# Gate fold in column groups, last rows of the busiest expert in token order, second layer as nested arms, new sort keys

## Chip, cores and metric

One NeuronCore of a Trainium2 chip. The metric is the device time of one launch in microseconds (us); the kernel before has a median of 461.15 us over 3 runs (461.02 to 465.25).

## The reference

A block-sparse attention (2 batches, 8 heads, 768 positions, head size 64) gives 1536 token rows of 512 values. Two layers follow:

```python
def _moe_ref(x, w1, w2, w3, w_out):
    h = np.maximum(np.maximum(x @ w1, x @ w2), x @ w3)      # 512 -> 768
    return h @ w_out                                        # 768 -> 512

def _moe2_ref(x, w_skip, w_gate, w1, w2):
    do_compute = x @ w_skip > 0
    out = x.copy()
    e_idx = np.argmax(x @ w_gate, axis=1)                   # one of 8 experts
    gate_w = softmax(x @ w_gate)[chosen]
    for e in range(8):                                      # rows of expert e that compute
        h = np.maximum(x[mask] @ w1[e], 0.0)                # 512 -> 1024
        out[mask] = x[mask] + gate_w * (h @ w2[e])          # 1024 -> 512
```

On the inputs as drawn, the reference sends 1379 tokens to the busiest expert, 130 to a second one and 14 to a third; 13 skip the second layer. Of the 1379, 1252 lie ahead of the last 128 tokens.

## The kernel before, in words

**First stage (0 to 296 us of the span).** The 1536 tokens are worked in four groups `u` of 384. For each group there is attention over four head pairs (scores on PE, L301; softmax on DVE, ACT and POOL; transposes, L340; product with v, L353), then 18 `chain`s (L412: 12 matmuls of 384 columns each, three for each of six column blocks `f` of the hidden layer, from high and low parts of weights and input), their maximum on DVE (`chained`, L421), a split into high and low parts (`h_high` on ACT, `h_low` on POOL), and `x2_mm` (L439), which gives the 512 outputs and, in ten more columns, the logits of the second layer's gate. For these ten columns w_out is multiplied by the gate's weights beforehand, for each of six blocks `f` of w_out: `fold_t` transposes the block (L477), `fold_c` copies it to SBUF, `fold_mm` multiplies it with `w9` (L488: four matmuls of 10 columns in true float32, which are 8 passes in the trace), `fold_h` and `fold_l` split the result into the two weights.

The order of all of this is made by `arrange`, a list scheduler that runs when the kernel is built: each operation has an engine, a duration, dependencies, buffers, and a key from the table `KEYS`; of what is ready on an engine, that with the smallest key goes next. `HOME` says which copies run on another engine than ACT. Three PSUM buffers (`pm`) are shared by the chains, `x2_mm`, the folds and the routing. The 16 chunks of the first expert's weights are split into high and low parts on ACT (L774) and DVE (L776) at the end of this stage.

**Routing.** `route`, `route2`, `route3` find for each token its expert, its gate weight and its slot in a table in DRAM (`table`, CAP rows for each expert); `guess` picks the busiest expert from the counts of the first three groups.

**Second layer (296 us to the end).** The busiest expert's tokens are worked in `pair`s of two tiles of 128 rows, gathered by indirect DMA from `x2d`, and scattered to `out` by indirect DMA (`end`, L1108, POOL). `pair(0, 0)` and `pair(0, 1)` run under `tc.If(EA > EARLY)` (L1233). Beside the first of them DVE works `steps()` of `plan()`: some fifty small instructions on one partition that give the numbers of tiles, the experts' order and the rows to gather, for the registers of the engines. After the two arms of that If have joined, a second If (L1315) picks `most()` (one large expert, a few small ones) or `any_ranks()` (anything else). `most()` runs `pair(0, b0 + 1, 1)` and `pair(0, b0 + 2, FAST2)`, which carry the up to 32 left-over rows of two small experts as `tail`s (matmuls with a 32-column weight in four column groups, L1063 and L1074), then by `If`s on the count VK[0] further pairs (L1298, L1300), a `single` tile of 128 rows for an odd count (L1302) and a `single` of the second expert (L1304).

On these inputs the trace shows five pairs and two singles, twelve scatters in all: 11 tiles of the busiest expert and one of the second, in that order the last two being `single(0, l0)` and `single(1, b1 + 1)`. `single` has a first layer of 24 matmuls of 512 columns (L1185), transposes of the hidden rows (L1191), and a second layer of 24 matmuls of 512 columns (L1215); after it `end(1)` multiplies by the gate weight and adds the token row (L1105) and scatters.

Of the kernel before, what the change touches and what calls it, by code (L numbers as in the profile page):

```python
# [42 lines left out]
MAXT = NT  # L43
NRAW = 4
NCON = 293
# [7 lines left out]
KIND = dict(ch=0, cp=0, x2m=0, sc=1, pv=2, tu=3, st=3, ft=3, fm=1, wu=5)  # L53
PORTED, SWITCH = 0.5, 0.06

KEYS = dict(
    s=[[92.73, -181.27, -146.9, -16.72], [12.35, 16.72, 8.44, 74.05], [153.96, 186.16, 209.64, 168.62],
       [133.34, 186.33, 278.0, 31.35]],
    t=[[-48.88, -30.72, -72.46, -64.96], [-115.16, -107.84, -74.91, -96.18], [166.13, 294.76, 153.99, 200.69],
       [231.34, 228.77, 194.22, 148.78]],  # L60
    o=[[-192.26, -99.49, -155.84, -140.77], [18.47, 16.47, 41.51, 37.81], [199.26, 186.19, 169.77, 161.26],
       [233.93, 202.13, 203.99, 188.4]],
    v=[[-76.04, -20.69, -43.67, -52.86], [-21.73, 66.33, 25.77, 62.78], [184.33, 170.84, 129.72, 69.28],
       [217.41, 88.27, 101.06, 155.42]],
    d=[[-190.77, -106.26, -79.61, -70.3], [14.18, 17.1, 46.42, 50.54], [166.48, 205.9, 182.89, 208.26],
       [219.14, 230.09, 253.13, 240.15]],
    e=[[-118.48, -161.65, -267.53, -240.31], [-154.8, -98.57, -105.32, -102.62], [120.29, 131.21, 115.09,
       112.64], [172.38, 173.49, 165.52, 214.6]],
    c=[[23.72, 3.57, 54.8, 22.22, 44.87, 43.88, 88.26, 54.59, 86.07, 36.89, 6.99, -26.57, -32.31, 15.28,
# [5 lines left out]
    x=[-95.61, 258.36, 184.11, 502.78],  # L75
    w=[18.99, -6.3, 51.7, 43.13, 14.1, 99.04, 74.8, 61.7, 81.52, 99.86, 64.82, 35.29, 63.01, 76.52, 58.72,
       87.44, 90.17, 111.95, 78.35, 139.2, 88.06, 51.57, 155.3, 161.2],
    l=[-91.01, -34.87, 30.81, -0.24, -49.37, 13.11, 15.41, -9.33, 19.62, 18.83, 49.47, 74.71, 132.91, 84.56,
       70.49, 102.42, 139.84, 87.62, 100.63, 192.14, 145.35, 197.7, 185.22, 170.88],
    f=[61.9, 116.3, 154.03, 120.79, 115.82, 130.96],  # L80
# [11 lines left out]
def arrange(ops, room, keys):  # L92
# [46 lines left out]
    while len(order) < len(ops):  # L139
# [13 lines left out]
        for e in free:  # L153
            while free[e] <= now + 1e-9 and ready[e]:
# [7 lines left out]
                if e == "PE":  # L162
                    begin += SWITCH if kind not in (None, KIND.get(k, 4)) else 0.0
                    kind = KIND.get(k, 4)
# [29 lines left out]
def build(tc, a, out):  # L194
# [975 lines left out]
    def single(p, t, spl=0, last=False, hr=HR):  # L1170
# [31 lines left out]
        for f in range(8):  # L1202
            wh, wl = M2["w", p, 8 + f]
            i, o = f // 4, f % 4 * P
            if f == 2:
                turn_h(1)
                if not last:
                    turn_x()
# [171 lines left out]
```

## Time and profile before

| | |
|---|---|
| median of 3 runs | 461.15 us |
| profiled execution | 461.57 us, span 459.8 us |
| PE busy | 436.2 us, 95% of the span |
| DVE, ACT, POOL busy | 239.1, 187.7, 146.8 us |
| mean granted clock of TensorE | 0.988 of full speed |
| first stage / second layer | 0 to 296 / 296 to 459.8 us |

The span is the time between the first and the last recorded instruction; 1.8 us of the profiled execution lie outside of it. A matmul's end is modelled, so the pace of PE is read from the starts of consecutive matmuls. "Idle before" is time in which an engine had nothing to run, with the event that ended it.

### The profile page before, as it was taken

The numbers are of one execution on the slowest core, as the hardware profiler recorded it, in microseconds if no ns is written. First come the engines' busy times: TensorE is split into PE (matmuls) and PEld (weight loads), VectorE is DVE, ScalarE is ACT, GpSimd is POOL, SyncE is SP. The second block draws the span as 40 slices with busy tenths as digits, with TensorE's granted clock in tenths as the row PEclk, the third lists the DMA queues.
The fourth block names the chain that finished last, engine by engine and source line by source line (L and its number), as shares of the span: only waits on it lengthen the run. The fifth ranks groups of instructions, "written<-read, shape, count | busy, mean of one in ns | idle before, by whom it ended". The sixth has DMA issues, their size and how long they took to land. (4 is left out here: it accounts for less than half of the span.)

```text
span 459.8 us, 9575 instructions
## 1 busy us (share of the span) xinstructions
PE 436.2 (95%) x3523; PEld 392.3 (85%) x3523; DVE 239.1 (52%) x708; ACT 187.7 (41%) x505; POOL 146.8 (32%) x199
## 2 busy tenths in 40 slices
PE   6999899999999899999999998999989999999992
PEld 2767789999999898999999997999969889798881
DVE  3689899999832833325204168575136551323220
ACT  2688886555462767623211065211115511111220
POOL 2464456325121532104400251142224043231230
PEclk9799999999999999999999999999999999999998
DMA  8964635678203444501012074324911381010100
GB/s 253 296 223 138 228 117 184 210 239 265 70 17 138 144 86 143 177 16 47 2 61 78 2 265 150 137 45 120 341 49 50 94 301 68 19 50 20 55 18 29
DMA packets 27670, 56.85 MB, mean 124 GB/s; under 512 B 6463, under 2 KB 8767, under 8 KB 27608
## 3 DMA queue, kind: packets, MB, share of 16 engines
q1 hardware_dynamic: 24808, 49.71, 33.3%
q0 software_dynamic: 2800, 6.37, 4.4%
q8 instruction: 32, 0.52, 0.6%
q14 instruction: 30, 0.25, 0.2%
HBM read 46.95 MB, written 10.47 MB: 125 GB/s over the span
## 5 line engine op out<-in xcount | busy, mean ns | idle before, releaser
L412 PE MATMUL pm<-xh,wh 128*128 128x384 f32 x288 | 65.4, 347 | 1.3 <-DVE t L421 1.1
L412 PE MATMUL pm<-xl,wh 128*128 128x384 f32 x288 | 62.4, 336 | 0.3 <-DVE xl L364 0.3
L412 PE MATMUL pm<-xh,wl 128*128 128x384 f32 x288 | 62.4, 336 | 0.0
L412 PEld LDWEIGHTS pm<-xh,wh 128*128 128x128 f32 x288 | 49.6, 188 | 3.6 <-DVE t L421 2.1
L1133 ACT ACTIVATE hth<-ph 128x256 fp32r<-128x256 f32 x40 | 15.4, 385 | 89.6 <-PE ph L1130 82.2
L412 PEld LDWEIGHTS pm<-xl,wh 128*128 128x128 f32 x288 | 51.2, 188 | 0.7 <-DVE xl L364 0.7
L412 PEld LDWEIGHTS pm<-xh,wl 128*128 128x128 f32 x288 | 51.2, 188 | 0.0
L1134 DVE SCALAR_TENSOR_TENSOR htl<-ph,hth 128x256 fp32r<-128x256 f32 x40 | 16.8, 423 | 61.9 <-ACT hth L1133 60.8
L439 PE MATMUL pm<-wh,h 128*128 128x262 f32 (+1 forms) x288 | 42.3, 287 | 1.9 <-ACT h L426 0.7
L335 POOL TENSOR_TENSOR pr<-pr,se 128x360 f32<-128x360 f32 x32 | 26.5, 845 | 55.2 <-DVE se L331 44.8
L421 DVE TENSOR_TENSOR t<-pm,t 128x384 f32<-128x384 f32 x48 | 26.4, 551 | 31.8 <-PE pm L412 22.7
L325 ACT ACTIVATE pr<-pr,mx 128x120 f32<-128x120 f32 x96 | 36.6, 384 | 14.6 <-DVE mx L318 14.5
L439 PEld LDWEIGHTS pm<-wh,h 128*128 128x128 f32 x288 | 38.0, 189 | 2.9 <-ACT h L426 0.9
L429 POOL TENSOR_TENSOR h<-t,h 128x384 fp32r<-128x384 f32 x24 | 26.2, 1099 | 35.3 <-ACT h L426 26.7
L756 POOL DMA_INDIRECT xn<-x2d,inx x16 | 17.7, 1103 | 52.5 <-DVE xm L1096 24.2
L1142 PE MATMUL pm<-wh,hth 128*128 128x512 f32 x80 | 31.8, 397 | 0.0
L1142 PE MATMUL pm<-wh,htl 128*128 128x512 f32 x80 | 31.5, 393 | 0.0
L1142 PE MATMUL pm<-wl,hth 128*128 128x512 f32 x80 | 31.3, 391 | 0.0
L600 POOL DMA_INDIRECT table<-rtab,rsi x12 | 12.0, 1001 | 54.6 <-DVE g_m L617 20.9
L1130 PE MATMUL ph<-xth,wh 128*128 128x256 f32 x160 | 26.3, 286 | 2.1 <-issue 2.1
L1130 PEld LDWEIGHTS ph<-xth,wh 128*128 128x128 f32 x160 | 23.1, 188 | 4.6 <-issue 2.9
L388 POOL TENSOR_SCALAR cx<-cx 128x512 f32<-128x512 f32 x24 | 19.2, 803 | 21.4 <-ACT cx L384 21.1
(295 smaller groups left out, 847.8 us busy)
## 6 DMA issues: line engine op xcount, KB each, us to landing
raw<-in_m SPq DMA_DIRECT2D x48, 256.0 KB
raw<-in_wx SPq DMA_DIRECT2D x22, 512.0 KB
vx<-in_vx SPq DMA_DIRECT2D x14, 288.0 KB
qt<-in_qt SPq DMA_DIRECT2D x16, 192.0 KB
raw<-in_vt SPq DMA_DIRECT2D x8, 384.0 KB
x2d<-raw SPq DMA_DIRECT2D x12, 256.0 KB
kx<-in_kx SPq DMA_DIRECT2D x8, 360.0 KB
out<-raw SPq DMA_DIRECT2D x9, 256.0 KB
```

Source lines behind the costliest of these rows:

```text
L325: nc.scalar.activation(pr[:, t, :], pr[:, t, :], AF.Exp, bias=mx[:, t:t + 1], scale=-1.0, accum_out=se[:, h, t:t + 1])
L335: nc.gpsimd.tensor_tensor(pr, pr, ST["se", u, p][:, h].unsqueeze(2).broadcast_to([P, TPG, KT]), ALU.mult)
L388: nc.gpsimd.tensor_scalar(x, x, HIGH, LOW, ALU.min, ALU.max)
L412: nc.tensor.matmul(ST["ch", u, f, j], l[j, f][:, c * P:(c + 1) * P], r[u][:, c, :], start=(cs[0] == 0 and n == 0), stop=(cs[-1] == KC1 - 1 ...
L421: nc.vector.tensor_tensor(ST["t1", u, f], ps, ST["t1", u, f], ALU.max)
L429: nc.gpsimd.tensor_tensor(HL[u, f], ST["t1", u, f], HH[u, f].bitcast(F32), ALU.subtract)
L439: nc.tensor.matmul(ps, l[u, f][:, t * P:(t + 1) * P], r[3, f][:, lo:hi], start=(part != 1 and n == 0), stop=(part != 0 and n == len(ops) - 1))
L756: nc.gpsimd.indirect_dma_start(out=xn[t], out_offset=None, in_=x2d, in_offset=bass.IndirectOffsetOnAxis(ap=inx[:, t, 0:1], axis=0), bounds ...
L1130: nc.tensor.matmul(ps, w[:, o:o + P], r[:, d, :], start=(n == 0), stop=(n == 3 * KC1 - 1))
L1133: nc.scalar.activation(hh, ps, AF.Relu)
L1134: nc.vector.scalar_tensor_tensor(hl, ps, 0.0, hh.bitcast(F32), ALU.max, ALU.subtract)
L1142: nc.tensor.matmul(py[i], l[:, o:o + P], r, start=(f == 0 and n == 0), stop=(f == 7 and n == 2))
```

## The change

Four parts, and a table of numbers.

1. `fold_mm` multiplies in four column groups of 32: each of the four pieces of the contraction writes its own 32 rows of one PSUM tile (128 columns). `fold_s` copies that to SBUF on ACT, and `fold_q` adds the four pieces by one matmul with the constant `pick9`. `fold_h` and `fold_l` follow as before.
2. The last 128 tokens are a tile in SBUF already. Where leaving them out of the count of the busiest expert saves a tile, the last tile of that expert is replaced by these 128 tokens in token order (`dense`): they are transposed during the second expert's `single`, all 128 are computed, a mask (by slot) sets the gate weight to zero for those that the regular tiles hold, and two plain stores of 256 columns write the rows. The rows of `out` are read first. The table's steps on DVE grow for it.
3. `most()` stands inside the first If, behind `pair(0, 1)`; one word (`ints[:, 6 * NE:]`) holds all that its arms need, and the arms are nested, each with its own copy of what follows, so that one path through them lies in a row. `any_ranks()` stands in the program twice.
4. New `KEYS` and `HOME`; in the scheduler's model a change of PE from one kind of work to another costs more.

Core of the diff (the tables are shown by one line each):

```diff
-    o=[[-192.26, -99.49, -155.84, -140.77], [18.47, 16.47, 41.51, 37.81], [199.26, 186.19, 169.77, 161.26],
+    o=[[-117.16, -89.93, -97.28, -83.95], [25.53, 37.54, -54.69, 32.04], [110.79, 140.86, 128.76, 119.48],
...
-    ("c4", "Pool"): [0, 1, 3, 6, 8, 9, 14, 17, 21, 22, 23],
-    ("fv", "Pool"): [(0, 1), (0, 2), (0, 3)],
+    ("c4", "Pool"): [0, 2, 6, 8, 9, 18, 20, 21],
+    ("fv", "Pool"): [(0, 0), (0, 1), (0, 2), (0, 3)],
+    ("ph", "DVE"): [(0, 0), (1, 1)],
...
     def fold_mm(f):
         pg = psM.tile([P, 512], F32, name="pm")
         for c in range(KC1):
-            nc.tensor.matmul(pg[:, :NG9], ST["ft", f][:, c * P:(c + 1) * P], w9[:, c, :], start=(c == 0),
-                             stop=(c == KC1 - 1))
+            nc.tensor.matmul(pg[32 * c:32 * c + 32, :P], con[:, c * NG9:c * NG9 + 32], ST["ft", f][:, c * P:(c + 1) * P], start=True, stop=True)
+    def fold_s(f):
+        nc.scalar.copy(ST["ft", f][:, :P], ST["fg", f][:, :P])
+    def fold_q(f):
+        ST["fg", f] = ST["fg", f][:, 2 * P:]
+        nc.tensor.matmul(ST["fg", f][:, :NG9], ST["ft", f][:, :P], pick9, start=True, stop=True)
...
+    def turn_d():
+        nc.vector.memset(yq[:1], 1.0)
+        for c in range(KC1):
+            o = slice(c * P, (c + 1) * P)
+            nc.tensor.transpose(ptx[0][:, o], X2[NG - 1, TPG - 1][:, o], ident)
+    def put_d():
+        src = ptx[0].rearrange("p (c k) -> p c k", k=P)
+        nc.scalar.copy(xth[:, :, :P], src)
+        nc.vector.tensor_tensor(xtl[:, :, :P], src, xth[:, :, :P].bitcast(F32), ALU.subtract)
+    def gate_d():
+        nc.tensor.matmul(pq[:, :2], yq[:1], ONE["lim"], start=True, stop=True)
...
+    def second_d(z, f):
+        wh, wl = M2["w", 0, 8 + f]
+        h, o = f // 4, f % 4 * P
+        for n, (l, r) in enumerate(((hth[h], wh), (hth[h], wl), (htl[h], wh))):
+            nc.tensor.matmul(py[z][:, halves[z]], l[:, o:o + P], r[:, halves[z]],
+                             start=(f == 0 and n == 0), stop=(f == 7 and n == 2))
+    def end_d():
+        rows = out[B * S - P:, :]
+        nc.sync.dma_start(xr[1], rows)
+        for z, cs in enumerate(halves):
+            for f in range(4, 8):
+                second_d(z, f)
+            nc.vector.scalar_tensor_tensor(yo[0][:, cs], py[z][:, cs], gd[1], xr[1][:, cs], ALU.mult, ALU.add)
+            nc.sync.dma_start(rows[:, cs], yo[0][:, cs])
...
-        with tc.If(VK[0] > 6):
-            pair(0, b0 + 3)
-            with tc.If(VK[0] > 8):
-                pair(0, b0 + 4)
-        with tc.If((VK[0] & 1) == 0):
-            single(0, l0, hr=M2["raw"])
-        with tc.If(VK[1] > 1):
-            single(1, b1 + 1, last=True, hr=M2["raw"])
+        def last():
+            with tc.If((w & DENSE) > 0, preferred_fallthrough_block=True) as dense:
+                single(1, b1 + 1, last=True, hr=M2["raw"], then=True)
+                single(0, 0, last=True, hr=M2["raw"][2:], dense=True)
+            with dense.Else():
+                with tc.If((w & ONES) > 0):
+                    single(1, b1 + 1, last=True, hr=M2["raw"])
+        def odd():
+            with tc.If((w & 1) > 0, preferred_fallthrough_block=False) as one:
+                single(0, l0, hr=M2["raw"])
+                last()
+            with one.Else():
+                last()
+        with tc.If((w & (ONES - 1)) > 5, preferred_fallthrough_block=True) as four:
+            pair(0, b0 + 3)
+            with tc.If((w & (ONES - 1)) > 7, preferred_fallthrough_block=False) as five:
+                pair(0, b0 + 4)
+                odd()
+            with five.Else():
+                odd()
...
+    with tc.If(EA > EARLY, preferred_fallthrough_block=True) as early2:
+        with tc.manual_schedule():
+            pair(0, 0, gen=steps())
+            numbers()
+            pair(0, 1)
+            word = reg(ints[:, 6 * NE:], 2 * OTHER - 1)
+            with tc.If(word >= OTHER, preferred_fallthrough_block=False) as others:
+                any_ranks()
+            with others.Else():
+                most(word)
```

How the instructions move. On PE, what stands between the end of `pair(0, 1)` (or of the other arm) and the first matmul of the next pair, before: the last matmul of the pair, a jump over the whole other arm (whose last rows are the two transposes and two jumps), then the loads of registers and the second If.

```order
L1142 MATMUL pm<-wh_5_3761,htl_3982 128x512
L1233 UNCONDITIONAL_BRANCH
...
L743 MATMUL ptx_3488<-ident,xn_3490 128x128 x4
L1240 UNCONDITIONAL_BRANCH
L1233 UNCONDITIONAL_BRANCH
L732 TENSOR_LOAD p_ints
L1315 COMPARE_AND_BRANCH
L732 TENSOR_LOAD p_ints x2
L1130 MATMUL ph_3484<-xth,wh_0_3535 128x256
```

The same place now, word for word in a row of the program:

```order
L1185 MATMUL pm<-wh_5_3771,htl_4000 128x512
L772 TENSOR_LOAD p_ints
L1411 COMPARE_AND_BRANCH
L1173 MATMUL ph_3516<-xth,wh_0_3569 128x256
L1173 MATMUL ph_3516<-xth,wh_0_3650 128x256
```

One load and one compare are left, and no jump. The second place is PE behind `pair(0, b0 + 3)`, before (with the jumps that end the Ifs behind the pair that isn't run):

```order
L1142 MATMUL pm<-wh_5_3761,htl_3982 128x512
L1300 UNCONDITIONAL_BRANCH x2
L1298 UNCONDITIONAL_BRANCH
L1302 REGISTER_ALU
L1302 COMPARE_AND_BRANCH
L1185 MATMUL ph_3484<-wh_0_3535,xth 128x512
```

and now (L1266 is the first layer of the second expert's `single`):

```order
L1185 MATMUL pm<-wh_5_3771,htl_4000 128x512
L1389 REGISTER_ALU
L1389 COMPARE_AND_BRANCH
L1381 REGISTER_ALU
L1381 COMPARE_AND_BRANCH
L1373 REGISTER_ALU
L1373 COMPARE_AND_BRANCH
L1266 MATMUL ph_3516<-wh_5_3928,xth 128x512
```

Three compares stand here, and the arm that this word selects follows them directly. The third place is DVE at the end of the first stage (L421, now L424, is the maximum that frees a chain's PSUM buffer; L776, now L816, the split of the next layer's weights). Before:

```order
L776 TENSOR_TENSOR wl_2_3640<-raw_3472,wh_2_3639 128x512
L421 TENSOR_TENSOR t_3611<-pm,t_3611 128x384
L776 TENSOR_TENSOR wl_2_3662<-raw_3473,wh_2_3661 128x512
L776 TENSOR_TENSOR wl_3_3668<-raw_3474,wh_3_3667 128x512
L421 TENSOR_TENSOR t_3611<-pm,t_3611 128x384
L776 TENSOR_TENSOR wl_3_3689<-raw_3475,wh_3_3688 128x512
```

and now:

```order
L816 TENSOR_TENSOR wl_0_3655<-raw_3500,wh_0_3654 128x512
L424 TENSOR_TENSOR t_3137<-pm,t_3137 128x384
L816 TENSOR_TENSOR wl_1_3663<-raw_3501,wh_1_3662 128x512
L816 TENSOR_TENSOR wl_1_3669<-raw_3502,wh_1_3668 128x512
L816 TENSOR_TENSOR wl_2_3674<-raw_3503,wh_2_3673 128x512
```

The last maximum now stands ahead of the fifth split; before, it stood ahead of the eleventh.

## Rows read from the trace of the kernel before

**Rows 1.** Windows: 29 to 100 us (length, busy time and count of each engine, clock, DMA)

```profile
29.00:100.00 71.00, 68.78 (x611) 60.34 (x610) 65.76 (x160) 53.21 (x138) 34.19 (x40) 1.00 0.53 178
```

**Rows 2.** Waits of PE, 20 to 296 us (sum in us, times, longest)

```profile
PE pm L412 <- DVE t L421: 1.1, 3, 0.8
...
PE pm L439 <- ACT h L426: 0.7, 1, 0.7
```

**Rows 3.** Timeline of PE: a fold, a tail (start, duration, idle before)

```profile
94.43 0.95 PE L488 MATMUL pm<-con,cr 128*128 128x10 f32 x8
95.24 0.94 PE L412 MATMUL pm<-xh,wh 128*128 128x384 f32 x4
...
370.32 0.40 PE L1142 MATMUL pm<-wh,htl 128*128 128x512 f32 x1
370.70 1.95 PE L1074 MATMUL pm<-raw,hqt 128*32 128x128 f32 x64
372.58 0.74 PE L1130 MATMUL ph<-xth,wh 128*128 128x256 f32 x4
```

**Rows 4.** Timeline of PE at three places with a branch

```profile
294.89 0.88 PE L439 MATMUL pm<-wh,h 128*128 128x262 f32 x6
295.61 0.64 PE L1130 MATMUL ph<-xth,wh 128*128 128x256 f32 x4
296.09 0.64 PE L1130 MATMUL ph<-xth,wl 128*128 128x256 f32 x4
...
342.20 0.40 PE L1142 MATMUL pm<-wh,htl 128*128 128x512 f32 x1
344.74 0.71 PE L1130 MATMUL ph<-xth,wh 128*128 128x256 f32 x4 [2.15 <-issue]
...
424.36 0.40 PE L1142 MATMUL pm<-wh,htl 128*128 128x512 f32 x1
425.75 0.47 PE L1185 MATMUL ph<-wh,xth 128*128 128x512 f32 x1 [0.99 <-DVEq L1300]
```

**Rows 5.** The chain that ended last: two of its pieces (start, us, what)

```profile
446.31 0.44 PE ph L1191 x4
446.75 4.14 PE pm L1215 x18
```

**Rows 6.** Timeline, the last instructions

```profile
450.48 0.39 PE L1215 MATMUL pm<-mw_15h,htl 128*128 128x512 f32 x1
450.96 0.75 DVE L1105 SCALAR_TENSOR_TENSOR yo<-pm,ic,xr 128x512 f32<-128x512 f32 x1 [2.83 <-PE pm L1215]
452.52 0.99 POOL L1108 DMA_INDIRECT out<-yo,isc  x1 [8.95 <-DVE yo L1105]
```

**Rows 7.** Windows at the end (columns as in rows 1)

```profile
454.75:455.00 0.25, 0.00 (x0) 0.00 (x0) 0.00 (x0) 0.00 (x0) 0.00 (x0) 1.00 0.13 33
```

**Rows 8.** Closing instructions: ns min/median/max, first and last start

```profile
L1376 POOLq DRAIN  x3: 40/109/3841, 455.1 to 459.5; - x3
L1376 SPq DRAIN  x3: 7/7/13, 456.5 to 459.2; - x3
```

**Rows 9.** A plain store: the copy ahead, its issue, the window of its first bytes

```profile
289.90 0.38 ACT L463 COPY x<-pm 128x262 f32<-128x262 f32 x1
...
290.31 0.35 SPq L456 DMA_DIRECT2D out<-x  x1
...
291.00:291.50 0.50, 0.50 (x7) 0.50 (x6) 0.50 (x1) 0.35 (x1) 0.00 (x0) 1.00 0.68 246
```

**Rows 10.** DVE: the plan's first step, the splits behind it; a matmul that waits

```profile
300.88 0.14 DVE L669 TENSOR_TENSOR p_ci<-pm,g_ad 1x8 int32<-1x8 f32 x1
...
311.53 0.74 DVE L1134 SCALAR_TENSOR_TENSOR htl<-ph,hth 128x256 fp32r<-128x256 f32 x2
...
316.75 0.39 PE L1142 MATMUL pm<-wh,htl 128*128 128x512 f32 x1
```

**Rows 11.** DVE where the first stage ends

```profile
274.05 2.30 DVE L776 TENSOR_TENSOR wl<-raw,wh 128x512 fp32r<-128x512 f32 x1 [0.21 <-ACT wh L774]
```

More of the change, by code (lines that the diff above doesn't have):

```diff
@@ L162, in arrange @@
                 if e == "PE":
-                    begin += SWITCH if kind not in (None, KIND.get(k, 4)) else 0.0
-                    kind = KIND.get(k, 4)
+                    last, kind = kind, KIND.get(k, 4)
+                    if last not in (None, kind):
+                        begin += SWITCH + (SHORT if kind != 0 and last not in (0, 5) else 0.0)
                     end = begin + matmuls(k, begin, o["dur"])
@@ L568, in route2 @@
         if u == NG - 1:
-            ST["cnt"] = counts(ACC[NG])
+            ST["cnt"] = counts(ACC[NG], ST["part"])
         oh, ohb, do, w, tab = ST["rt", u]
@@ L601, in scatter, with counts @@
                                      in_=tab[:, j, :], in_offset=None, bounds_check=NROW - 1, oob_is_err=False)
-    def counts(acc):
+    def counts(*accs):
         pc = psM.tile([P, 512], F32, name="pm")
-        nc.tensor.matmul(pc[:1, :NE], ones[:, :1], acc, start=True, stop=True)
-        return pc[:1, :NE]
+        for i, acc in enumerate(accs):
+            nc.tensor.matmul(pc[:1, i * NE:(i + 1) * NE], ones[:, :1], acc, start=True, stop=True)
+        return pc[:1, :NE * len(accs)]
     def count3():
@@ L1033, in build @@
     yq = mp.tile([P, P], F32, name="yq")
+    gd = [z.bitcast(F32) for z in (mo[:, 0:1], mo[:, 1:2], mi[:, 0:1])]
     xq, xqt = (M2["spare"][:, i * P:(i + 1) * P] for i in range(2))
@@ L1208, in single @@
                     turn_x()
+                elif then:
+                    turn_d()
                 splits(4)
+            if dense and f == 4:
+                end_d()
+                return
             if f == 3:
@@ L1212, in single @@
                     next_x(t + 2)
+                elif then:
+                    put_d()
+                    gate_d()
                 splits(4)
+            if dense:
+                for z in range(2):
+                    second_d(z, f)
+                continue
             for n, (l, r) in enumerate(((hth[i], wh), (hth[i], wl), (htl[i], wh))):
@@ L1230, in numbers @@
             raw_load(c, reg(ints[:, NE + 1:NE + 2], NE - 1, **SP))
-    take_x()
-    with tc.If(EA > EARLY) as early2:
-        with tc.manual_schedule():
-            pair(0, 0, gen=steps())
-            numbers()
-            pair(0, 1)
-    with early2.Else():
-        ids("in2", reg(ONE["r0"], NROW - 2 * P, **SP))
-        with tc.If(EA > 0) as early:
-            with tc.manual_schedule():
-                pair(0, 0, gen=steps())
-        with early.Else():
-            for _ in steps():
-                pass
-            advance(row(1))
-            turn_x()
-            next_x(2)
-        numbers()
     VK, EK, BK, LK, MR = {}, {}, {}, {}, {}
@@ L1285, in run_rank, with most @@
                 run_rank(k + 1)
-    def most():
-        for k in range(2):
-            VK[k] = reg(ints[:, k:k + 1], MAXT + 1)
+    def most(w):
         b0, b1, l0 = (reg(ints[:, i * NE + k:i * NE + k + 1], 14, **SP) for i, k in ((2, 0), (2, 1), (3, 0)))
@@ L1312, in any_ranks @@
         run_rank(0)
-    with tc.manual_schedule():
-        with tc.If(reg(ints[:, 6 * NE:], MAXT) > 0, preferred_fallthrough_block=False) as others:
+    take_x()
+    with tc.If(EA > EARLY, preferred_fallthrough_block=True) as early2:
[8 more added lines that the diff above has]
+                most(word)
+    with early2.Else():
+        ids("in2", reg(ONE["r0"], NROW - 2 * P, **SP))
+        with tc.If(EA > 0) as early:
+            with tc.manual_schedule():
+                pair(0, 0, gen=steps())
+        with early.Else():
+            for _ in steps():
+                pass
+            advance(row(1))
+            turn_x()
+            next_x(2)
+        numbers()
+        with tc.manual_schedule():
             any_ranks()
-        with others.Else():
-            most()
     ctx.close()
```

130 lines of the change are left out of this document (87 added, 43 removed), and 11 rows, old and new, of tables (HOME, c).

## The prediction

> **What bounds the kernel now.** I read the table of busy time first: PE is the busiest engine by far, in both stages. So the question is where PE stands still or does work that can go, and what lies behind its last matmul. Then the waits of PE in the first stage: behind 20 us they are short, and two of the longest, 0.8 and 0.7 us [rows 2], lie at its end, where a last chain waits for a PSUM buffer and the output waits for the split hidden rows. In the timeline of PE through the second layer only two waits are long: 2.15 us where `pair(0, 1)` ends and the arms of the first If join, and 0.99 us behind the third pair of `most()`, where the pair that isn't run is jumped over [rows 4]. The rest is the end: from the modelled end of the last matmul, 450.87, to the end of the span, 459.80, are 8.93 us in which PE has nothing [rows 6]. These three places and the folds are where the change works. All sums below are made against the profiled execution, 461.57 us (span 459.8); the median of the runs is 0.42 us lower, and the result is moved by that.
>
> **Fold.** A `fold_mm` takes 0.81 us of PE now (94.43 to 95.24, 8 passes of 0.10) [rows 3]; six are 4.9 us. New are 8 passes with a 32-column weight and 128 columns; the tails run just these: 64 in 1.88 us (370.70 to 372.58), 0.03 each, so 0.24 us [rows 3]. `fold_q` is 2 passes of the old form, 0.20 us. Together 0.44, six times 2.6 us. Going into column groups costs something: the tail's first matmul starts 0.38 us behind the last 512-column one, whose pace is 0.23 [rows 3, 5], so 0.15; behind the tail I see no loss. The new order has four groups of `fold_mm` (two of them double); with 0.15 in and as much out I put 1.2 us on it, though the way out showed nothing. That gives 3.84 against 4.86: -1.0 us. Bounds: -2.2 (free switches) and +0.8 (the added ACT copy holds up PE at every fold by 0.3 us). A copy of 262 columns takes ACT 0.38 us [rows 9]; six smaller ones are at most 2.3 us, hidden beside ACT's idle 18 us from 29 to 100 us [rows 1] and as much later, since the scheduler has put chains or transposes between `fold_mm` and `fold_q`. [...]
>
> **The branches.** The jump over the other arm goes; a load of one register and a compare stay. At 294.89 to 295.61 PE passes just such a load and compare (EA, L1233) with nothing lost: six matmuls at 0.12 fill the 0.72 us [rows 4]. So I expect the 2.15 us to go but for 0.1. Behind the third pair stand three compares, all falling through on these inputs: the word's low part is 6 (eleven tiles, less the four of the first two pairs, less the dense one), so the pair is run, the next is not, no odd single, and the dense arm is taken. -0.9 of 0.99. Together -3.0 us. Bounds: -3.1, and -1.0 if loads and compares, not the jump, were two thirds of the gaps. What is late next: the pair's inputs are split two matmul groups before it, the weights' splits wait for nothing new.
>
> **The dense tile.** The tiles are as many as before: 1252 tokens ahead of the last 128 make 10 tiles, 1379 make 11, so one single becomes dense and goes last. PE loses the 8 transposes of the next tile (twice 0.44 [rows 5]) and gets 4 (0.44), a tiny matmul for the mask (0.1), and its second layer as 48 matmuls of 256 columns at 0.12 [rows 4] in place of 24 of 512 at 0.23 [rows 5]: 5.76 against 5.52. Sum -0.1 us (from -0.5 to +0.5). The read of `out` waits for the second expert's scatter; by the old end, its bytes land 4 us behind the last matmul [rows 6, 7], and the read row is needed when the first half's matmuls are done, 24 * 0.23 + 0.88 + 5.76 - 1.44 = 10.7 us behind it: hidden, with 6 us for the read. On SP only the two stores stand behind it.
>
> **The plan.** DVE gets 22 more small steps beside `pair(0, 0)`. The 51 of now take at most the time from 300.88 to 311.53 [rows 10], 0.21 each, so 22 are 4.6 us at the most. The split that then stands behind the plan (0.37) would end at 316.5, and its matmul comes at 316.75 [rows 10]: nothing, by 0.25 us at the worst. If that cover failed, PE would wait the excess once, 0.5 to 1 us. The gather of the next rows on POOL and the second expert's weights on SP's queue come later by as much; these are worked on in the third pair, behind 344.74 [rows 4], 28 us behind the plan: nothing.
>
> **The end.** Now: DVE starts 0.09 us behind the last matmul, takes 0.75, POOL starts the scatter at 452.52, ends it at 453.51 [rows 6], the last bytes go by 454.8 [rows 7], SP is through its waits at 456.5, but POOL's closing drain lasts 3.84 us, to 458.94 [rows 8], and 0.86 us later the span ends. Then: 0.09, half a row on DVE 0.40 (a split of 256 columns: 0.37 [rows 10]), 0.03 to SP's issue, 0.85 from issue to first byte (290.31 to 291.16, from the share 0.68 of its window), 128 KB at 362 GB/s 0.36 [rows 9]: last byte at 1.73 us. If SP again needs 1.7 us behind the bytes and POOL's drain is long over, its last scatter being some 10 us earlier, 0.86 more make 4.3: -4.6. If the drain stays 3.84 us behind the last byte whatever it was, 1.73 + 0.3 + 3.84 + 0.86 = 6.7: -2.2. I take -4.2, near the first, since the drain is POOL's and so is the scatter ahead of it. SP's own closing jump now comes behind its last store, where before SP had jumped 20 us earlier. By the gap at the join it costs 2.15 us; beside the store's flight (0.35 issue + 2.15 against 0.35 + 2.6) it is hidden. [...]
>
> **Keys.** At the end of the first stage DVE has a split that takes 2.30 us [rows 11] where a neighbour with half the columns takes 0.37 [rows 10], and a chain's maximum behind it; this makes the 0.8 us wait. The new order sets the last maximum ahead of eleven splits, not five. The wait of 0.7 us, the chain of maximum, ACT and POOL behind the last chain, can't all go. -0.8 us (0 to -1.5). For the rest of the first stage no view tells which order is better: two copies move to DVE and three of 512 columns to ACT (by the 0.38 us for 262 columns [rows 9] some 1.1 and 2.3 us), DVE is busy 65.76 of 71 us where the weights are converted, and PE has 2.2 us idle there [rows 1]. 0, with 2.5 us either way.
>
> **Sum.** -1.0 - 3.0 - 0.1 - 4.2 - 0.8 = -9.1 us: 452.5 for such an execution, 452.1 as a median. With all the good ends (-2.2, -3.1, -0.5, -4.6, -1.5, -2.5) 446.8; with all the bad ones (+0.8, -1.0, +0.5, -2.2, 0, +2.5) 461.8.
>
> **Rivals.**
> The close stays: POOL's drain or SP's jump in series. For: the drain is long and nobody else was late. Against: its place behind the scatter. 2.0 us less: 454.1.
> A fold now holds one of three PSUM buffers from `fold_mm` to `fold_l` over two more steps; double folds leave one buffer to the chains, and the shifted homes delay conversions. For: three of PE's waits are for buffers or DVE already. Against: there are two such places, at 0.8 us each. 1.6 us there and 2.5 elsewhere: 456.2.
> The dense arm isn't taken, if the count falls otherwise: its 4.3 us go, and one jump of 1 us comes: 457.4. Against: the counts above.
> Slower: the conversions of the 24 weight blocks between 29 and 100 us become what PE waits for. Price: if each of them comes 0.8 us later than PE wants it, 19 us: 471.3. It decides from 9.1 us on, 0.4 us per block. For: DVE is 93% busy there [rows 1]. Against: PE's order has chains of two groups to choose from, and the moved copies are 3.4 us in all.
>
> **How the numbers follow.** Forecast 0.62, its own range 447 to 455; the close stays 0.15; buffers 0.16; no dense arm 0.03; slower 0.04. About 1% (4.6 us) is what a measurement here can tell from no change; the line is 456.5. The forecast, the close and the better half of the buffer case lie below: 0.85. Within 1%: the rest of that and no dense arm: 0.11. Slower: 0.04. The range 446.5 to 457.5 leaves out some 0.1 above and little below.
>
> **What would show it.** PE without a gap over 0.3 us at the end of `pair(0, 1)` and ahead of the two singles; `fold_mm` at 0.24 us for 8 passes; the span ending 4 to 5 us behind the last matmul, POOL's long drain not last; the dense tile's 48 matmuls at 0.12 without a wait; the waits at the end of the first stage near 1 us in sum. It is wrong if the first matmul of the second layer comes later than 295 us, if compares show gaps, or if the end still takes over 6 us.

## The result, and the profile after

The changed kernel takes 456.23 us (median of 6 runs, 453.81 to 456.79) beside 461.53 us for the kernel before (6 runs); the ratio is 0.987, with a 95% interval from 0.982 to 0.992. That is faster by 1.3%, or 5.3 us between the medians, inside the range given (446.5 to 457.5), and 4.1 us above the time named. A ratio counts only the runs within 1.5% of the fastest of their kernel; where it leaves out a third of them or more, the median of all is given too. The profiled execution takes 455.98 us, its span is 454.2. It was forecast at 452.5; here is where the difference lies:

| part of the span | before | after | change | forecast |
|---|---|---|---|---|
| start to first matmul of the second layer | 295.61 us | 297.62 us | +2.0 | -1.8 |
| from there to the end of the last matmul | 155.26 | 150.99 | -4.3 | -3.1 |
| from there to the end of the span | 8.93 | 5.59 | -3.3 | -4.2 |

The second layer gained a little more than forecast, the end a little less, and the first stage, where a small gain was forecast, lost 2 us.

**The branches.** The timeline of PE at the first two places of [rows 4], now:

```profile
343.87 0.39 PE L1185 MATMUL pm<-wh,htl 128*128 128x512 f32 x1
344.09 0.64 PE L1173 MATMUL ph<-xth,wh 128*128 128x256 f32 x4
...
422.61 0.39 PE L1185 MATMUL pm<-wh,htl 128*128 128x512 f32 x1
422.84 0.40 PE L1266 MATMUL ph<-wh,xth 128*128 128x512 f32 x1
...
432.39 0.38 PE L1225 MATMUL pm<-p_kc,yq 1*128 1x2 f32 x2 [0.46 <-DVE yq L1214]
```

The first matmul of the third pair comes 0.22 us behind the last of the second, the first of the single 0.23 us behind the last of the pair: PE's own pace. The waits of 2.15 and 0.99 us are gone. The last row is new: the tiny matmul for the dense tile's mask waits 0.46 us for a row of ones that DVE sets just ahead of it.

**The end.** First the last instructions (timeline), then windows (columns as in [rows 1]), then the closing instructions as in [rows 8]:

```profile
448.33 0.28 PE L1238 MATMUL pm<-wh,htl 128*128 128x256 f32 x1
448.65 0.48 DVE L1247 SCALAR_TENSOR_TENSOR yo<-pm,mo,xr 128x256 f32<-128x256 f32 x1 [0.95 <-PE pm L1238]
```

```profile
450.25:451.00 0.75, 0.00 (x0) 0.00 (x0) 0.00 (x0) 0.00 (x0) 0.00 (x0) 1.00 0.35 108
451.00:453.00 2.00, 0.00 (x0) 0.00 (x0) 0.00 (x0) 0.00 (x0) 0.00 (x0) 0.68 0.02 4
```

```profile
L1487 POOLq DRAIN  x3: 40/109/3568, 442.1 to 453.9; - x3
L1487 SPq DRAIN  x3: 7/7/13, 453.3 to 453.6; - x3
...
L1373 SPq COMPARE_BRANCH  x1: 43/43/43, 449.8 to 449.8; - x1
...
L1487 SPq EVENT_SEMAPHORE  x8: 27/28/28, 452.5 to 453.0; - x8
```

POOL's long drain, 3.57 us, now starts at 442.1 and is over long before the end. The last bytes go by 451.0. But SP, which left its arm at 449.8, shows its next instruction only at 452.5, and its first drain at 453.3; the span ends 0.9 us later, as before.

**The first stage.** The waits of PE from 20 to 296 us, to be read against [rows 2], and the timeline of PE and of ACT at the longest:

```profile
PE pm L415 <- ACT t L422: 2.2, 1, 2.2
PE sc L304 <- issue: 1.3, 1, 1.3
PE pm L442 <- POOL h L432: 1.0, 1, 1.0
...
PE pm L442 <- ACT x L464: 0.8, 1, 0.8
```

```profile
45.60 0.86 PE L415 MATMUL pm<-xh,wl 128*128 128x384 f32 x4
48.66 1.44 PE L415 MATMUL pm<-xh,wh 128*128 128x384 f32 x4 [2.20 <-ACT t L422]
...
44.33 0.38 ACT L328 ACTIVATE pr<-pr,mx 128x120 f32<-128x120 f32 x1
...
45.59 0.83 ACT L292 COPY vx<-v 24x768 f32<-24x768 f32 x1
46.45 0.40 ACT L328 ACTIVATE pr<-pr,mx 128x120 f32<-128x120 f32 x1
...
47.60 0.65 ACT L383 ACTIVATE cr<-raw 128x512 int32<-128x512 uint32 x1
48.16 0.45 ACT L422 COPY t<-pm 128x384 f32<-128x384 f32 x1
```

Three chains have run by 46.46 us and hold the three PSUM buffers. ACT, which must empty one, has the softmax of two heads, a copy of 0.83 us and the first step of a weight block ahead of that copy (L422), and is busy without a break (4.95 of the 5.00 us from 44 to 49). PE stands for 2.2 us. What follows is in the windows (the last three numbers are the granted clock, the share and the GB/s of the DMA engines):

```profile
46.00:48.75 2.75, 0.55 (x4) 0.23 (x2) 2.68 (x7) 2.73 (x10) 0.29 (x1) 1.00 0.65 231
48.75:52.50 3.75, 3.75 (x13) 3.69 (x14) 1.89 (x3) 2.73 (x5) 3.20 (x4) 0.54 0.71 234
```

PE was busy for 0.55 of 2.75 us; then the granted clock is 0.54 of full speed over 3.75 us, and four matmuls of a chain take 1.24 us from start to next start (48.66 to 49.90), where four ahead of the wait take 0.69 (44.91 to 45.60). By one less the granted clock nearly half of these 3.75 us is lost again: some 1.7 us, an estimate. With the 2.2 us of the wait the place costs 3.9 us. Near the start the two kernels don't differ in this: both have such waits and a low clock behind them. The first 30 us, of the kernel before and then of the changed one:

```profile
0.00:30.00 30.00, 25.52 (x258) 15.97 (x259) 18.58 (x74) 17.01 (x58) 12.84 (x26) 0.89 0.90 269
```

```profile
0.00:30.00 30.00, 24.92 (x242) 14.38 (x244) 18.62 (x74) 13.64 (x52) 12.61 (x27) 0.89 0.87 261
```

The first chain begins at 31.03 us now, before at 28.90; but six more matmuls of 512 columns (L237) stand ahead of it, 1.6 us that come later in the kernel before, and only 0.6 us more are waits. Over the whole first stage PE is idle for 13.8 us instead of 11.2, and the lower clock takes 5.1 us instead of 3.4 (one less the granted clock, summed over windows of 0.5 us).

**The fold.** Its rows in the timeline of PE (L491 is `fold_mm`, L499 `fold_q`):

```profile
124.55 0.65 PE L491 MATMUL pm<-cr,con 128*32 128x128 f32 x16
125.13 0.96 PE L415 MATMUL pm<-xh,wh 128*128 128x384 f32 x4
...
127.32 0.51 PE L499 MATMUL pm<-con,cr 128*128 128x10 f32 x4
127.68 0.85 PE L343 MATMUL pt<-ident,pr 128*120 128x128 f32 x6
```

Read from start to next start, the four groups of `fold_mm` take 2.2 us (here 0.58 for 16 passes) and the four of `fold_q` 1.15 (here 0.36 for 4): 3.3 us, against 3.84 forecast and 4.86 before.

### The profile page after: what moved, and what is told of

It is laid out like the page before. It is cut to its first block, busy times and chain, and to the rows that moved or that the text cites. A ratio compares the mean times of both kernels' runs of the same rounds, so it can differ in the third digit from the quotient of the medians.

```text
span 454.2 us, 9646 instructions
## 1 busy us (share of the span) xinstructions
PE 434.3 (96%) x3558; PEld 390.7 (86%) x3558; DVE 239.8 (53%) x737; ACT 187.6 (41%) x510; POOL 140.6 (31%) x189
## 4 chain that ended last, share of the span: by engine, by line
PE 67%; DVE 11%; DMA 7%; ACT 5%; issue 4%; POOL 2%; SPq 2%; POOLq 0%; DVEq 0%; ACTq 0%
PE pm L415 18%; PE ph L1173 13%; PE pm L1185 12%; PE pm L442 10%; ACT pr L328 3%; PE ph L1266 2%; DVE cx L396 2%; DMA raw<-in_wx 2%; DVE wl L408 2%; DMA table<-rtab,rsi 2%; DVE cx L395 2%; PE po L356 2%; PE pt L343 1%; POOL pr L338 1%; SPq L808 1%
## 5 line engine op out<-in xcount | busy, mean ns | idle before, releaser
L424 DVE TENSOR_TENSOR t<-pm,t 128x384 f32<-128x384 f32 x48 | 26.5, 554 | 46.7 <-PE pm L415 34.7
L338 POOL TENSOR_TENSOR pr<-pr,se 128x360 f32<-128x360 f32 x32 | 28.0, 896 | 25.0 <-DVE se L334 10.4
L614 POOL DMA_INDIRECT table<-rtab,rsi x12 | 12.0, 998 | 62.9 <-DVE g_m L632 20.6
L796 POOL DMA_INDIRECT xn<-x2d,inx x14 | 15.1, 1081 | 42.9 <-DVE xm L1139 28.2
L1173 PE MATMUL ph<-xtl,wh 128*128 128x256 f32 x160 | 25.3, 279 | 0.0
```

Source lines behind the costliest of these rows:

```text
L338: nc.gpsimd.tensor_tensor(pr, pr, ST["se", u, p][:, h].unsqueeze(2).broadcast_to([P, TPG, KT]), ALU.mult)
L424: nc.vector.tensor_tensor(ST["t1", u, f], ps, ST["t1", u, f], ALU.max)
L796: nc.gpsimd.indirect_dma_start(out=xn[t], out_offset=None, in_=x2d, in_offset=bass.IndirectOffsetOnAxis(ap=inx[:, t, 0:1], axis=0), bounds ...
L1173: nc.tensor.matmul(ps, w[:, o:o + P], r[:, d, :], start=(n == 0), stop=(n == 3 * KC1 - 1))
```

## The experiments

Ratios are to the kernel before, measured beside each on the same chip, with 95% intervals. The chips differ from that of the result: the kernel before had medians of 464 to 465 us on them.

**The first stage of before under the second layer of after.** The keys, homes, scheduler figures and the fold go back (a few of the lines):

```diff
-    f=[48.35, 98.8, 110.61, 104.21, 90.78, 122.35],
+    f=[61.9, 116.3, 154.03, 120.79, 115.82, 130.96],
...
-    ("ph", "DVE"): [(0, 0), (1, 1)],
...
-        op(("fm", f), "PE", 0.3, t + 0.2, fold_mm, f, after=[("fc", f), ("consts",)], take=[("pm", ("fm", f))])
+        op(("fm", f), "PE", 0.9, t + 0.2, fold_mm, f, after=[("fc", f), ("consts",)], take=[("pm", ("fm", f))], uses=[("fc", f)])
```

> The changed kernel with the first stage of the kernel before: its table of keys, its homes, its scheduler figures and its fold; the second layer stays as changed. On PE the first stage is then that of before but for one matmul of 8 columns. Theory A (the loss lies in the new order of the first stage): the second layer begins at 295.6 us instead of 297.6, its 151.0 us and the end of 5.6 us stay, so 456.2 - 2.0 = 454.2 us. Theory B (the second layer's gain depends on when it begins, or the 2 us are the spread of single executions): 456 us, no difference to the changed kernel that can be measured.

Measured 0.974 (0.970 to 0.979), below what theory A asked (0.984); this counts three of its six runs, and the median of all six, 456.58 beside 465.05, gives 0.982. Since it and the changed kernel had run on different chips, it was run again beside the changed kernel itself.

> The changed kernel once more, on the chip of the three runs beside it, so that they are compared with it directly and not over the kernel before. Ratio to the kernel before near 0.987, as measured.

> The changed kernel with the whole first stage of the kernel before (keys, homes, scheduler figures, fold), once more beside the changed kernel. If the new order of the first stage costs what the first batch showed, it is 3 to 6 us below the changed kernel, with the second layer beginning 2 us earlier or more; if that was the spread of that chip, within 1 us of it.

The changed kernel again 0.987 (0.980 to 0.993), median 457.61 us; with the old first stage 0.981 (0.975 to 0.986), median 454.44. In the profiles the second layer begins at 302.20 and 296.17 us. So theory A holds: under one and the same second layer the new first stage is the slower one, by 2.8 us between the ratios, by 3.2 between the medians. The two intervals overlap, so the size is loose.

This second profile of the changed kernel has a wait that the first one had only as 0.28 us. Timeline of PE, of SP's queue and of POOL, then windows:

```profile
158.56 0.39 PE L304 MATMUL sc<-kx,qt 64*64 64x120 f32 x2 [1.25 <-issue]
...
160.23 1.65 PE L415 MATMUL pm<-xh,wh 128*128 128x384 f32 x4
...
173.75 1.48 PE L304 MATMUL sc<-kx,qt 64*64 64x120 f32 x24 [3.52 <-DMA qt<-in_qt]
...
165.61 0.33 SPq L279 DMA_DIRECT2D vx<-in_vx  x1
...
166.47 0.42 SPq L273 DMA_DIRECT2D qt<-in_qt  x1
...
164.28 1.01 POOL L614 DMA_INDIRECT table<-rtab,rsi  x1 [1.49 <-DVE se L334]
```

```profile
166.00:170.00 4.00, 4.00 (x51) 3.79 (x49) 1.02 (x2) 3.51 (x7) 2.64 (x4) 1.00 0.66 38
170.00:174.00 4.00, 0.48 (x7) 0.30 (x10) 0.70 (x2) 0.00 (x0) 0.24 (x1) 0.91 0.97 302
174.00:180.00 6.00, 6.00 (x40) 5.70 (x37) 1.90 (x15) 2.86 (x13) 1.26 (x2) 0.50 0.20 63
```

The load of `qt`, issued at 166.47, lands 7.3 us later. From 166 to 170 the DMA engines are 66% busy and move 38 GB/s; the bytes come behind that, and after PE's wait the clock is 0.50 for 6 us. In the first profile the same load (166.84) landed in 5.2 us, and the same stretch shows 0.66 at 137 GB/s. What differs is the order: there the routing's scatter of 128 rows of 8 bytes (L614) starts at 166.74, behind the loads' first issue; here it starts 1.3 us ahead of it. The seven profiles with the new first stage divide by this: four have the scatter 1.3 to 1.4 us ahead and this wait at 3.2 to 4.1 us, three have it behind the first issue and wait 0.2 to 1.1 us. Four with the old first stage wait 1.6 to 2.2 us for `qt` there, in two pieces, the kernel before 0.34.

The same four differ from the three even earlier. All seven have the wait of 1.25 us near 160 us (L304); behind it the granted clock falls to 0.50 in these four and stays at 1.00 in the three. Here four matmuls of a chain take 1.65 us at 160.23, in the first profile 0.97 at 162.74, and the loads are issued later for it. So the order of scatter and loads may itself come from the clock. That the scatter delays the loads is read from these rows; no run took it or the wait of 1.25 us away.

The second layer begins at 302.1 to 303.8 us in the four, and at 296.7 to 297.6 in the three. With the old order it begins at 295.0 to 296.2 in three profiles and at 301.6 in a fourth, in which the lower clock took 8.5 us of the first stage. The wait near 47 us is fixed and what follows it is not: it stands in all seven with 2.0 to 2.2 us, and the clock falls behind it in three of them. So one profile doesn't price the new order: by the means, the second layer begins some 2 us later in its good profiles than in the good ones of the old order, and some 7 us later in the others.

**The two halves crossed.** New fold with the old keys, and old fold with the new keys (the scheduler then builds an order of its own in each):

> Keys, homes and scheduler figures of before, but the new fold, whose copy and second matmul go first on their engines as soon as they can. Theory A (the fold gains, the new order of all the rest loses): the fold's gain of the trace of after, 48 matmuls of 10 columns at 0.10 us gone, 48 of 128 columns in a column group at 0.03 to 0.05 and 12 of 10 at 0.1 added, is 1.4 us in all; 454.2 - 1.4 = 452.8 us. Theory B (the fold holds PSUM buffers and makes PE wait, which eats what it saves): 454.2 us or more, with waits of PE at L415 or L480 next to the folds.

> The new keys, homes and scheduler figures with the fold of before; the second layer as changed. Theory A: 456.2 + 1.4 = 457.6 us, with the wait of 1.8 us near 13 us of the span and the one of 2.2 us near 48 us still there, since neither is at a fold. Theory B (the fold is what costs): 454 to 455 us, and those waits gone.

Measured 0.990 (0.987 to 0.993) and 0.997 (0.994 to 1.0005). Neither theory: each table of keys is slower with the other's fold than with its own, by 0.9 to 1.6%. The wait of 1.83 us near 13 us of the span and one of 2.28 near 47 were there in the new order with the old fold as well, so the fold doesn't make them. As a measure of the fold the two are of no use, since a changed duration moves hundreds of instructions. So:

**The new fold in the old order, word for word.**

```diff
-        op(("fh", f), "ACT", 0.07, t + 0.3, fold_h, f, after=[("fm", f), ("c4",) + w])
+        op(("fh", f), "ACT", 0.07, t + 0.3, fold_qh, f, after=[("fm", f), ("c4",) + w])
...
+    def fold_m(f):
+        fold_mm(f)
+        fold_s(f)
+
+    def fold_qh(f):
+        fold_q(f)
+        fold_h(f)
```

> As the run beside it with the first stage of before, but with the new fold put where the old one stands: DVE and POOL keep their order word for word, ACT gets six copies of 128 columns, PE has other matmuls at the six folds and nothing else moved. Theory A (the fold by itself gains what its matmuls save): 4.9 us of matmuls against 2.2 + 1.2 us in the trace of after, so 1.5 us below the run with the old fold. Theory B (the fold's longer chain over ACT, and the PSUM buffer it holds, make PE wait, as the 460.4 against 453.2 of the first batch would say): level with the run with the old fold or above it, with waits of PE behind the folds.

0.983 (0.978 to 0.988), against 0.981 with the old fold: no gain. The timeline of PE shows why (L489 is `fold_mm` here, L497 `fold_q`):

```profile
93.19 0.43 PE L489 MATMUL pm<-cr,con 128*32 128x128 f32 x8
93.54 0.96 PE L413 MATMUL pm<-xh,wh 128*128 128x384 f32 x4
...
126.23 0.39 PE L497 MATMUL pm<-con,cr 128*128 128x10 f32 x2 [0.43 <-ACT cr L493]
...
130.26 0.39 PE L497 MATMUL pm<-con,cr 128*128 128x10 f32 x2 [0.49 <-ACT cr L493]
```

A fold with chains around it goes from 0.80 to 0.35 and 0.13 us. But the old order has five of the six folds within 10 us, with little between them, and there PE waits for the new copy on ACT. From the first transpose of that cluster to the first matmul of `x2_mm` the old fold takes 12.44 us (119.62 to 132.06), the new one 13.10 (119.67 to 132.77). Theory B, at these two places.

**The end.** The dense tile's rows by one scatter instead of two stores; the dense tile left out; the stores issued by ACT:

```diff
-            nc.sync.dma_start(rows[:, cs], yo[0][:, cs])
+        nc.gpsimd.indirect_dma_start(out=out, out_offset=bass.IndirectOffsetOnAxis(ap=ST["rt", NG - 1][4][:, TPG - 1, 0:1], axis=0),
+                                     in_=yo[0], in_offset=None, bounds_check=B * S - 1, oob_is_err=False)
```

> The changed kernel, but the rows of the dense tile are written by one indirect scatter on POOL behind the second half, as the last tile was before, not by two plain stores on SP. Theory A (the end is shorter because no scatter and no closing drain of POOL stands behind the last matmul): the end goes from 5.6 us back to that of before, 8.9 us, less 0.3 us because only half a row is left for DVE: 456.2 + 3.0 = 459.2 us, with a POOL drain of 3.5 us or more as the last long thing. Theory B (the end is set by jumps and waits that any last write meets): within 1 us of the changed kernel, 456.2 to 457.2 us.

```diff
-            V.tensor_tensor(dn, dn, is0, ALU.mult)
+            V.tensor_scalar(dn, dn, 0.0, None, ALU.mult)
```

> The changed kernel with the saved tile's count set to zero, so that the arm of the dense tile isn't taken: the last two tiles are the odd single of the busiest expert and the single of the second, with a scatter, as before. From the first matmul of these two singles to the last the changed kernel takes 25.8 us, before 25.1; the end is 5.6 us against 8.9. Theory A (the dense tile pays by its end alone): 0.65 us less on PE, 3.3 us more behind it, so 2.7 us above the changed kernel, ratio to the kernel before near 0.993. Theory B (the end's gain comes from the nested arms): end below 7 us.

```diff
-            nc.sync.dma_start(rows[:, cs], yo[0][:, cs])
+            nc.scalar.dma_start(rows[:, cs], yo[0][:, cs])
```

> The changed kernel, but the dense tile's two stores are issued by ACT and not by SP, so that SP has long left the arms when the last bytes go. From the last matmul to the end of the span were 5.6 us, 2.4 of them between the last bytes at 450.9 us and SP's first closing drain at 453.3. Theory A (SP's jump out of the arms, behind its last issue, is in series with the end): SP's drain comes 1 to 2 us earlier, the end is 4 to 4.6 us. Theory B (it is the store's own completion): the end stays at 5.4 to 5.8 us.

The scatter gives 0.996 (0.992 to 1.000), no dense tile 0.995 (0.991 to 0.999), ACT's stores 0.982 (0.975 to 0.989; four of six runs, and 0.985 by the median of all six). From the last matmul to the end of the span the three profiles have 9.98, 10.29 and 4.63 us, where the changed kernel has 5.59. Without the dense tile it is more than the 8.93 of before, since POOL's drain starts 3.9 us behind the start of the scatter (449.47) and not 2.6. The closing drain of POOL with the scatter, that without the dense tile, and the closing instructions with ACT's stores:

```profile
L1488 POOLq DRAIN  x3: 40/109/3650, 461.9 to 466.2; - x3
```

```profile
L1487 POOLq DRAIN  x3: 40/109/3842, 453.4 to 457.9; - x3
```

```profile
L1487 SPq DRAIN  x3: 7/7/13, 457.0 to 457.9; - x3
...
L1487 ACTq DRAIN  x2: 8/44/80, 457.6 to 457.9; - x2
...
L1373 ACTq COMPARE_BRANCH  x1: 38/38/38, 454.8 to 454.8; - x1
```

A drain of 3.65 and 3.84 us is last again where a scatter is last: that is the end's gain, theory A of both. With ACT's stores the last bytes go by 456.0 and SP, long out of its arm, drains at 457.0, 3.2 us behind the last matmul (453.77) instead of 4.7. Now ACT is late: it leaves the arm at 454.8 and shows its next instruction at 457.6. So the engine that issues the last store shows nothing for 2.7 us (SP, 449.8 to 452.5 in the changed kernel) or 2.8 us (ACT, 454.8 to 457.6) behind its jump out of the arm, and this comes behind the issue. Theory A, at 4.6 us; that gain of 1 us is seen in the profile, the times are too spread to show it.

**The branches.** The second If behind the join again, with a short and with a long arm to jump over:

```diff
-            word = reg(ints[:, 6 * NE:], 2 * OTHER - 1)
-            with tc.If(word >= OTHER, preferred_fallthrough_block=False) as others:
...
+    word = reg(ints[:, 6 * NE:], 2 * OTHER - 1)
+    with tc.manual_schedule():
+        with tc.If(word >= OTHER, preferred_fallthrough_block=False) as others:
```

> The changed kernel, but the choice between the two ways through the rest stands behind the join of the first If's arms again, as before: on PE one jump more and nothing else between the end of the second pair and the third. Theory A (the jump over the other arm made the gap): a gap of 2.1 us comes back at the first matmul of the third pair (L1173), where the changed kernel has none, and the time is 2 us above the changed kernel's. Theory B (the loads and compares of registers made it): no gap over 0.3 us.

```diff
         numbers()
+        with tc.manual_schedule():
+            with tc.If(EA > 3):
+                any_ranks()
     word = reg(
```

> As the run with the choice behind the join, with one thing more: a copy of the general way through the rest stands at the end of the other arm, under a condition that doesn't hold on these inputs. PE executes the same instructions as there; only the jump out of the first arm now goes over some 9,800 instructions and not 152. There the jump took 0.41 us and no gap was left; before, a jump of 3.26 us, five waits, three loads and a compare stood in the place of the gap of 2.15. Theory A (a far jump is what costs: it eats the lead of PE's sequencer): the jump takes 3.3 to 3.8 us and PE stands still for 1.2 to 2 us at the first matmul of the third pair (L1173), 1.5 us more in all than with the short jump. Theory B (the two loads behind the compare, gone in both runs, made the gap of before): no gap over 0.3 us.

0.987 (0.983 to 0.992) and 0.989 (0.980 to 0.997). The jump of PE (L1405, the longer of the two) and the first matmul of the third pair, with the short arm, with the long one, and the jump of the kernel before (L1233):

```profile
L1405 PEldq COMPARE_BRANCH  x2: 95/250/406, 295.8 to 340.9; - x2
...
343.64 0.39 PE L1185 MATMUL pm<-wh,htl 128*128 128x512 f32 x1
343.87 0.64 PE L1173 MATMUL ph<-xth,wh 128*128 128x256 f32 x4
```

```profile
L1405 PEldq COMPARE_BRANCH  x2: 95/1954/3814, 301.1 to 346.3; - x2
...
351.26 0.69 PE L1173 MATMUL ph<-xth,wh 128*128 128x256 f32 x4 [1.95 <-DMA mi<-table]
```

```profile
L1233 PEldq COMPARE_BRANCH  x2: 95/1678/3262, 294.0 to 339.4; - x2
```

With the short arm the jump takes 0.41 us and no gap comes: theory A of that run falls, a short jump doesn't make one. (Its end is 6.58 us, 1.0 more than the changed kernel's: SP leaves the last arm at 449.8, 5.0 us ahead of the end of the span, where the changed kernel has 4.4.) Over some 9,800 instructions it takes 3.81 us, and the gap is 1.95 us, though loads and compare are the same. (The row names a DMA; PE's compare stands at 351.0, right ahead of the matmul.) Later a wait of 1.04 us follows for a gather, and the second layer takes 154.9 us instead of 150.8; its interval is too wide for the ratio to show it. So the gap follows the time of the jump, and between these two runs the jump differs in its target alone. The kernel before had the slow kind, 3.26 us, over an arm of the same length as the one passed in 0.41. The traces show these two kinds; why before was of the slow kind at that length no run here shows.

A slow jump nearly by itself is seen in the run without the dense tile. There the branch behind `pair(0, b0 + 3)` is taken, to the odd single, with no load of a register behind it and one semaphore step of 0.05 us:

```profile
L1381 PEldq COMPARE_BRANCH  x1: 3557/3557/3557, 419.1 to 419.1; - x1
...
422.78 0.47 PE L1266 MATMUL ph<-wh,xth 128*128 128x512 f32 x1 [0.88 <-issue]
```

It takes 3.56 us and PE stands for 0.88 us. So nested arms save the gap on the path that falls through and not on one with such a jump, and 0.9 us of what that run lost is this gap.

**The parts that held, together.** Old first stage and fold, nested arms, dense tile, stores on ACT, and the row of ones set before the single ahead:

> A version put together from the parts that held: first stage of the kernel before with its old fold, nested arms, dense tile, whose two stores are issued by ACT (the end was 4.6 us so instead of 5.6) and whose row of ones is set before the single ahead of it (the wait of 0.46 us of PE for it goes). 3.0 us from the first stage, 1.0 from the stores and 0.45 from the row of ones below the changed kernel: ratio to the kernel before 0.977. If the first stage's gain was the spread of the two chips, 0.984.

Measured 0.978 (0.972 to 0.984), median 452.01 us against 464.41 on that chip, as expected. The second layer begins at 294.99 us, PE waits nowhere in it, and the end is 4.59 us. It lies below the changed kernel (0.987), though the two intervals overlap; the run with the old first stage alone (0.974 and 0.981) isn't told apart from it.

## Why the prediction was right and where it was wrong

**By its own signs.** PE has no gap over 0.3 us at the end of `pair(0, 1)` and ahead of the two singles, the dense tile's 48 matmuls come at 0.12 us, POOL's long drain isn't last, and the end is under 6 us. Three sizes were missed: 0.35 us for 8 passes of `fold_mm` and not 0.24, an end of 5.6 us and not 4 to 5, waits of 1.8 us in sum at the end of the first stage and not near 1. And the first matmul of the second layer comes at 297.62 us, past the 295 that it set as a sign of being wrong. That the time still lies in the range is luck in part: the first stage came out 3.8 us worse than forecast and the end 0.9, the second layer 1.2 us better, and the upper bound is 1.3 us away.

**Fold (-1.0).** Right in its own rows, -1.5: the 0.15 us for going into column groups is about what a group of 8 passes takes over 0.24 (0.35). It paid where the order has a chain between its two halves (0.80 us to 0.35 and 0.13 in the old order). Over all of the old order it gains nothing, as the bad end of the bounds had it, by waits for ACT's copy (0.43 and 0.49 us).

**Branches (-3.0).** Right: -3.1 at the two places. The reason was half the story: the jumps of PE in these traces take either up to 0.41 us, which the lead of PE's sequencer hid (with the short arm the jump began at 340.9, 2.7 us ahead of the start of the pair's last matmul at 343.64), or 3.26 to 3.82 us, which used that lead up where work followed, so that waits, loads and compare behind it lay open. Before, the jump began at 339.4, 2.8 us ahead of the start of the pair's last matmul [rows 4], and the waits and loads behind it run from 342.7 to 344.5, right ahead of the matmul at 344.74. This explains the first place. At the second, before, the jump over the pair (L1300, at 421.6) shows 0.35 us, and PE's sequencer shows nothing more until 424.8; what held it there no run shows, and both gaps went with the nested arms.

**Dense tile (-0.1).** The two singles together went from 25.12 to 25.77 us. 0.46 of the 0.65 is the wait for the row of ones, a step that the sum left out; it went when the row was set earlier.

The second layer as a whole gained 1.2 us more than forecast. 0.36 of that is the wait of L1068, which this profile doesn't have; the rest is 0.2 us or so in each pair without a wait. Other profiles of the same second layer without new gaps take 150.6 to 151.8 us, so part of it is spread; the rest stays open.

**Plan (0).** Right. DVE's timeline, the plan's first step and the split behind its last:

```profile
302.82 0.15 DVE L686 TENSOR_TENSOR p_ci<-rw,g_ad 1x8 int32<-1x8 f32 x1
...
316.88 0.92 DVE L1177 SCALAR_TENSOR_TENSOR htl<-ph,hth 128x256 fp32r<-128x256 f32 x2
```

From the one to the other are 14.06 us, before 10.65 [rows 10]: the 22 steps take 3.4 us, at most 4.6 were forecast, and PE waits nowhere in that pair.

**The end (-4.2).** Right in kind, -3.3. The step that failed is that SP's closing jump is hidden beside the store's flight. By the trace it lies in series with SP's last waits: SP leaves its arm at 449.8, behind its last issue, and goes on at 452.5, some 1.5 us later than it would have (3.2 us behind the last matmul against 4.7, with the stores on ACT).

**Keys (-0.8, and 0 for the rest with 2.5 either way).** This is the step that failed. The waits at the end of the first stage hardly got shorter (1.0 and 0.8 us where 0.8, 0.7 and 0.6 stood), though the last maximum came ahead of the splits as the order promised (of twelve; the prediction counts eleven, and the 0.37 us that it sets beside the split of 2.30 are another operation's: splits of that size right behind take 0.67). And the rest isn't 0: with the fold's -1.5 taken out, the new order costs +3.5 us in the profile. 2.6 are more waiting of PE and 1.7 more time at the lower clock; 0.8 are gained in matmuls, which was not taken apart. The one place at 46 to 52 us holds 3.9 of these 4.3. The order as such told nothing of this, since it takes durations to see: three chains in a row against an ACT that is full from 44 to 49 us. The clock's part can't be read from an order either: other profiles of this one have the wait without the fall, and what decides it no run shows.

**Rivals.** The time is that of the buffer case (456.2), at another place than named: not a fold but three chains hold the buffers, and ACT empties them late; that the numbers agree is chance. Of the case in which the close stays, SP's jump in series came, at 0.9 us and not 2.0. The slow case was far off: the weight conversions made PE wait once, not at each block.

## What to carry to other kernels

An order made by a scheduler's model should be judged by its waits on the chip, stage by stage: where PE has as many results in flight as buffers, look at what stands ahead of the emptying copy on the other engine. A wait of PE of 2.2 us cost 3.9 us here with the fall of the granted clock to 0.54 behind it; read several profiles first, since behind the same wait the clock fell in three of seven. The rows of a program's last store belong in an order that needs no scatter (here an end of 5.59 us with two plain stores, 9.98 with a scatter), and its queue should be that of an engine that has little else to wait for at the end (5.59 us with SP's, 4.63 with ACT's); one that need not leave an arm at all was not tried.

## What was not expected of the hardware

A jump of PE's sequencer took 0.19 to 0.41 us or 3.3 to 3.8 us, nothing between; ahead of its matmuls by 2.8 us, the sequencer hides the one and not the other. SP and ACT, leaving the last arm, show 43 and 38 ns for the branch, and then no instruction for 2.7 and 2.8 us (SP 3.3 us in the run with the short arm). A scatter of 128 rows of 8 bytes, 1.3 us ahead of three loads on SP's queue, went with a load landing in 7.3 instead of 5.2 us. And the granted clock took waits of PE that look alike in two ways: behind 2.0 to 2.2 us near 47 us it fell to half in three profiles of seven and stayed at 1.00 in four, and behind the waits of 2.15 and 1.95 us ahead of the third pair (kernel before, long arm) it stayed at 1.00.
